# Attention by 512 tokens and four heads instead of 256 tokens and eight heads

## The chip, the cores and the metric

The kernel runs on one core of a Trainium2 chip. The metric is the device time of one execution in microseconds (us).

## What is computed

Attention in chunks of 64 tokens, then a mixture of experts whose router keeps state along the tokens:

```python
# q, k, v: [8 batches, 8 heads, 576 tokens, 64], chunks of 64 tokens
scores = q_c @ k_c.T / 8
attn   = softmax(scores, axis=-1)
x      = (attn @ v_c)  ->  [8, 576, 512]        # heads side by side
logits = x @ w_gate                             # 8 experts
gate   = sigmoid(x @ w_local)
# e = argmax(logits) where s == 0 or gate < 0.5, else the expert of the token before
out[b, s] = softmax(logits)[e] * (relu(x[b, s] @ w1[e]) @ w2[e])
```

## The kernel before

The work has two phases. The attention phase goes over 18 units of 256 tokens by 8 heads. Sixteen are regular (two per batch, tokens 0 to 511, `place`, L117); units 4 and 13 are leftovers, which collect the last 64 tokens of four batches. A unit goes through these steps:

- `load_qk` (L124) brings q and k to SBUF, two consecutive tokens of one head in a row of a partition, so that each contiguous run is 512 bytes; `load_v` (L138) brings v, one token of one head at a time, in runs of 256 bytes, two DMAs for a regular unit and four for a leftover.
- `pair_heads` (L151) copies q and k on GpSimd so that two heads lie side by side (tiles qr, kr).
- `qk_transposes` (L183) turns them with TensorE, four 128x128 blocks to a PSUM bank, and ScalarE moves each bank to qT or kT (L162).
- `scores` (L194): 64 small matmuls into sc; VectorE takes the maximum and subtracts it, ScalarE makes the exponential.
- `p_transposes` (L232), `values` (L241: 64 small matmuls and the division on VectorE), `x_transposes` (L278), each with two or more banks that ScalarE moves.
- `router` (L286): four matmuls for the logits, two transposes, and `red` (L305), which sums on VectorE, copies the nine logits beside x and writes the rows of x with them to DRAM (x_d; 521 floats, 2084 bytes a row).

The order is written out by hand: a string per unit ("steady", L62) names the steps of units at different stages, and each engine runs its part in that order. `lq` issues the load of q and k of unit i+5, `lv` that of v of unit i+1, both on the SP queue, which also carries x_d and the weights and works in order. v has two buffers (L115), so `lv` waits until `values` of unit i-1 has read its buffer. "start" (L41) and "drain" (L45) do the same for the first units and for the change to the second phase; the router's first half (`route`, L337) is hung into units 10 to 15.

The second phase gathers the rows of x by expert in tiles of 128 and runs two matrix multiplications per tile (L684, L705) with weights that are loaded by expert.

Of the kernel before, what the change touches and what calls it, by code (L numbers as in the profile page):

```python
# [32 lines left out]
LEFT = 4  # L33
EARLY = 3
# [27 lines left out]
    "steady": "lq s*8 s h0 tx*8 s va*4 va tq*8 ra*2 h1 tq*8 va*4 lv va ra*2 h2 tp*8 s pr*4 h3 ",  # L62
# [5 lines left out]
def tile_attention_then_moe(ctx: ExitStack, tc, q, k, v, wg, wl, w1, w2, out):  # L68
# [46 lines left out]
    vbuf = [pa1.tile([P, 2, H, DV], F32, name=f"v{i}") for i in range(NV)]  # L115

    def place(i):  # L117
        ph, j = divmod(i, 9)
        if j == LEFT:
            return 9 * ph + 8, [(4 * ph + n, 512, 64) for n in range(4)]  # L120
        j -= j > LEFT
        return 9 * ph + j, [(4 * ph + j // 2, 256 * (j % 2), 256)]

    def load_qk(i, parts=1):  # L124
        qt = pe2.tile([P, H, 2 * D], F32, name="qt", tag="qt", bufs=3)
        kt = pe2.tile([P, H, 2 * D], F32, name="kt", tag="kt", bufs=3)
        p0 = 0
        for b, s0, n in place(i)[1]:
            for h in range(0, H, H // parts):
                for dst, src in ((qt, q), (kt, k)):  # L130
                    nc.sync.dma_start(
                        dst[p0:p0 + n // 2, h:h + H // parts],
                        src[b, h:h + H // parts, s0:s0 + n, :].rearrange("h (p r) d -> p h (r d)", r=2),
                    )
            p0 += n // 2
        return qt, kt

    def load_v(i):  # L138
        vt = vbuf[i % NV]
        t0 = 0  # L140
        for b, s0, n in place(i)[1]:
            for s1 in range(s0, s0 + n, P):
                m = min(P, s0 + n - s1)
                nc.sync.dma_start(
                    vt[t0 % P:t0 % P + m, t0 // P, :, 0:D],
                    v[b, :, s1:s1 + m, :].rearrange("h s d -> s h d"),
                )
                t0 += m
        return vt

    def pair_heads(qk, engs):  # L151
        fns = []
        dsts = [pe2.tile([P, 4, 2, 2, D], F32, name=nm + "r", tag=nm + "r", bufs=1) for nm in "qk"]
        for n in range(2):
            sv = qk[n].rearrange("p (j h) (r d) -> p h j r d", j=2, r=2)
            for r in range(2):
                fns.append(lambda n=n, sv=sv, r=r: evac(engs[2 * n + r], dsts[n][:, :, r], sv[:, :, :, r]))
        return dsts, fns
# [24 lines left out]
    def qk_transposes(hd, qT, kT, engs=None):  # L183
        atoms = []
        fine, engs = engs is not None, engs or QK_ENG
        qkv = [t.rearrange("a h (p r) -> a h p r", r=2) for t in (qT, kT)]
        for m in range(2):
            for r in range(2):
                atoms += trans4(lambda n, m=m, r=r: hd[m][:, n, r].rearrange("p j d -> p (j d)"),
                                [(engs[2 * m + r], qkv[m][:, :, :, r], lambda ps: ps)], fine)  # L190
        return atoms


    def scores(qT, kT, pr, fine=False):  # L194
        sc = ps_s.tile([P, 2, 4, 2, D], F32, name="sc")

        def group(h, cc):
            for cp in range(2):
                ch = 2 * cp + cc
                for j in range(2):  # L200
                    nc.tensor.matmul(  # L201
                        sc[64 * cp:64 * cp + 64, j, h, cc, :],
                        qT[64 * j:64 * j + 64, h, 64 * ch:64 * ch + 64],
                        kT[64 * j:64 * j + 64, h, 64 * ch:64 * ch + 64],
# [36 lines left out]
    def values(pT, vt, xs, fine=False):  # L241
        box = {}

        def group(j, h):
            if h == 0:
                box["o"] = ps_o.tile([P, 2, 512], F32, name="o")
            o = box["o"]
            for cp in range(2):
                for cc in range(2):
                    nc.tensor.matmul(  # L250
                        o[64 * cp:64 * cp + 64, cc, DV * h:DV * h + D + 1],
                        pT[64 * cc:64 * cc + 64, 4 * j + h, 64 * cp:64 * cp + 64],
                        vt[64 * cc:64 * cc + 64, cp, 4 * j + h, 0:D + 1],
                        start=True, stop=True,
                    )
# [3 lines left out]
        def norm(j):  # L259
                ov = box["o"][:, :, 0:4 * DV].rearrange("p c (h d) -> p c h d", d=DV)  # L260
                rs = pa2.tile([P, 2, 4], F32, name="rs")
                nc.vector.tensor_scalar_add(rs, ov[:, :, :, D], 1e-9)
                nc.vector.reciprocal(rs, rs)
                nc.vector.tensor_tensor(
                    xs[:, :, 256 * j:256 * j + 256].rearrange("p c (h d) -> p c h d", d=D),
                    ov[:, :, :, 0:D],
                    rs.unsqueeze(3).to_broadcast([P, 2, 4, D]),
                    ALU.mult,
                )
# [8 lines left out]
    def x_transposes(xs, xT, fine=False):  # L278
        atoms = []
        for cc in range(2):  # L280
            atoms += trans4(
                lambda n, cc=cc: xs[:, cc, P * n:P * n + P],
                [(nc.scalar, xT[:, :, P * cc:P * cc + P], lambda ps: ps)], fine)
        return atoms

    def router(i, xT, xs, fine=False):  # L286
        lg = ps_l.tile([P, 2, 256], F32, name="lg")
        lT = pa2.tile([P, 256], F32, name="lT", bufs=1)

        def mm():  # L290
            for c in range(4):
                nc.tensor.matmul(lg[32 * c:32 * c + 32, 0], wg9[:, c], xT[:, c], start=True, stop=True)
# [6 lines left out]
        def tr():  # L299
            for cc in range(2):  # L300
                nc.tensor.transpose(lg[:, 1, P * cc:P * cc + P], lT[:, P * cc:P * cc + P], ident)
# [3 lines left out]
        def red():  # L305
            slot, rows = place(i)
            Lt = L[:, 2 * slot:2 * slot + 2, :]
# [3 lines left out]
            if len(rows) == 1:  # L311
                (b, s0, n), = rows
                nc.sync.dma_start(x_d[S * b + s0:S * b + s0 + n, :].rearrange("(c p) n -> p c n", p=P), xs)
            else:
                for m, (b, s0, n) in enumerate(rows):
                    nc.sync.dma_start(x_d[S * b + s0:S * b + s0 + n, :], xs[64 * (m // 2):64 * (m // 2) + 64, m % 2])
# [143 lines left out]
    def a_tq(i, engs=None):  # L460
        qkT[i] = (pe2.tile([P, 4, 256], F32, name="qT", bufs=1), pe2.tile([P, 4, 256], F32, name="kT", bufs=1))
        return qk_transposes(hd.pop(i), *qkT[i], engs)

    def a_pair(i, engs=(nc.gpsimd,) * 4):
        hd[i], fns = pair_heads(qk.pop(i), engs)
        return fns

    def a_sa(i, fine=False):
        prs[i] = pa2.tile([P, H, 2, D], F32, name="pr")
        return scores(*qkT.pop(i), prs[i], fine)  # L470
# [5 lines left out]
    def a_va(i, fine=False):  # L476
        xss[i] = pa2.tile([P, 2, XR], F32, name="xs", bufs=3)
        return values(pTs.pop(i), vts.pop(i), xss[i], fine)

    def a_tx(i, fine=False):  # L480
        xTs[i] = pa2.tile([P, 4, 256], F32, name="xT", bufs=1)
        return x_transposes(xss[i], xTs[i], fine)
# [27 lines left out]
    def constants():  # L510
# [10 lines left out]
        for ph in range(2):  # L521
            iota(None, [[9, 4], [4, 2], [2, 2]], base=36 * ph, dst=iota_t[:, TA * ph:TA * ph + TA - 2])
# [22 lines left out]
    for t in vbuf:  # L545
        nc.gpsimd.memset(t[:, :, :, D:DV], 1.0)
# [37 lines left out]
    def slots(pool, q0, q1, halves, qs, tags=({}, {}, {})):  # L584
# [35 lines left out]
        def s3():  # L620
# [9 lines left out]
            V.tensor_single_scalar(bits[:, 0], bits[:, 1], 64, ALU.bitwise_and)  # L630
# [483 lines left out]
```

## Time and profile before

| | us |
|---|---|
| three timed runs: median (lowest to highest) | 669.76 (669.27 to 671.48) |
| the profiled execution, its own time | 674.2 |
| its span, first to last instruction | 672.4 |
| PE busy, of the span | 638.5 (95%) |
| VectorE, ScalarE, GpSimd busy | 371.6, 271.6, 147.1 |

Attention takes about the first 160 us of the span. The profiled execution lies 4.4 us above the median of the timed runs. An engine's busy time is the union of its instructions' spans; the DMA share is the time of all packets over 16 engines, and can pass 1 because packets of one engine overlap.

### The profile page before, as it was taken

To read this page: it belongs to the slowest core of one execution; us is meant where nothing else is said; L and a number is where in the kernel's file an instruction comes from. 1 tells how busy PE (TensorE), PEld (TensorE's weight loads), DVE (VectorE), ACT (ScalarE), POOL (GpSimd) and SP (SyncE) were. 2 spreads that over 40 slices of the span, in tenths; PEclk is the share of its full clock that TensorE was granted. 3 is DMA by queue.
4 is the path that set the end of the run, shared out by engine and by line. 5 is a ranking of instruction groups with operands and counts; after the bars stand their busy time and mean duration, and the time that the engine had idled before them with its cause. 6 is when DMAs were issued, how large, how long until landed. Compare 5 with 4: busy or idle time off the path is not lost. (4 is left out here: it accounts for less than half of the span.)

```text
span 672.4 us, 16746 instructions
## 1 busy us (share of the span) xinstructions
PE 638.5 (95%) x5552; PEld 509.7 (76%) x5552; DVE 371.6 (55%) x938; ACT 271.6 (40%) x434; POOL 147.1 (22%) x209
## 2 busy tenths in 40 slices
PE   4889998889999999999999999999999999999993
PEld 4778776777787888678888886788888888678882
DVE  2656666976783766664332455762377432476231
ACT  4567676655312143542212433531465222342220
POOL 5323353560051111121121121121113121112101
PEclk9899999999999999999999999999999999999997
DMA  9999999977521144235121254452167411144101
GB/s 252 265 263 267 262 268 278 263 221 235 194 100 76 34 158 158 92 110 177 35 64 34 65 175 135 160 153 66 34 212 265 148 45 55 33 160 172 53 19 35
DMA packets 102505, 97.38 MB, mean 145 GB/s; under 512 B 42257, under 2 KB 79121, under 8 KB 102353
## 3 DMA queue, kind: packets, MB, share of 16 engines
q1 hardware_dynamic: 96192, 75.69, 38.8%
q0 software_dynamic: 6160, 19.85, 8.9%
q8 instruction: 73, 1.20, 0.7%
q14 instruction: 80, 0.65, 0.3%
HBM read 76.48 MB, written 19.56 MB: 143 GB/s over the span
## 5 line engine op out<-in xcount | busy, mean ns | idle before, releaser
L705 PE MATMUL y<-w2h,hp 128*128 128x512 f32 x560 | 185.3, 401 | 1.6 <-ACTq L992 1.2
L684 PE MATMUL h<-w1h,xp 128*128 128x512 f32 x560 | 164.3, 403 | 0.0
L771 POOL DMA_INDIRECT out<-ysb,sidx x38 | 43.7, 1151 | 374.0 <-DVEq L976 269.9
L705 PEld LDWEIGHTS y<-w2h,hp 128*128 128x128 f32 x560 | 105.0, 188 | 26.2 <-issue 2.5
L684 PEld LDWEIGHTS h<-w1h,xp 128*128 128x128 f32 x560 | 102.5, 189 | 21.8
L705 PE MATMUL y<-w2l,hp 128*128 128x512 f32 x280 | 110.5, 395 | 0.0
L753 ACT ACTIVATE hsb<-h 128x1024 f32<-128x1024 f32 x35 | 35.9, 1027 | 161.5 <-PE h L684 149.0
L684 PE MATMUL h<-w1l,xp 128*128 128x512 f32 x280 | 88.2, 396 | 0.7 <-DVEq L970 0.7
L652 ACT CAST hp<-tr 128x512 fp32r<-128x512 f32 x76 | 41.2, 589 | 108.1 <-PE tr L650 100.6
L653 DVE TENSOR_TENSOR xp<-tr,xp 128x512 fp32r<-128x512 f32 x39 | 27.0, 691 | 88.2 <-ACTq L970 56.9
L684 PEld LDWEIGHTS h<-w1l,xp 128*128 128x128 f32 x280 | 52.5, 188 | 14.2 <-DVEq L970 1.1
L705 PEld LDWEIGHTS y<-w2l,hp 128*128 128x128 f32 x280 | 52.6, 188 | 11.1
L653 DVE TENSOR_TENSOR hp<-tr,hp 128x512 fp32r<-128x512 f32 x76 | 49.3, 686 | 13.5 <-ACT hp L652 5.7
L1029 DVE TENSOR_SCALAR ysb<-y,ppr 128x512 f32<-128x512 f32 x31 | 23.3, 751 | 32.4 <-PE y L705 31.5
L650 PE MATMUL tr<-ident,hsb 128*128 128x128 f32 x304 | 40.2, 273 | 0.3 <-ACT hsb L753 0.3
L650 PEld LDWEIGHTS tr<-ident,hsb 128*128 128x128 f32 x304 | 35.3, 140 | 6.8 <-ACT w2h L954 1.2
L656 POOL DMA_INDIRECT xg<-x_d,gidx x36 | 35.4, 983 | 21.6 <-issue 9.8
L960 DVE TENSOR_TENSOR w2l<-raw,w2h 128x1024 fp32r<-128x1024 f32 x28 | 33.1, 1223 | 6.5 <-DVEq L943 5.2
L960 DVE TENSOR_TENSOR w1l<-raw,w1h 128x1024 fp32r<-128x1024 f32 x28 | 32.4, 1221 | 6.0 <-ACT w1h L954 5.2
L212 DVE TENSOR_REDUCE mx<-sc 128x8 f32<-128x512 f32 x36 | 23.2, 685 | 20.4 <-PE sc L201 20.4
L954 ACT CAST w2h<-raw 128x1024 fp32r<-128x1024 f32 x28 | 28.6, 1048 | 12.4 <-PE y L711 5.4
L250 PE MATMUL o<-v,pT 64*64 64x65 f32 x1152 | 27.7, 230 | 3.5 <-issue 2.1
(198 smaller groups left out, 833.8 us busy)
## 6 DMA issues: line engine op xcount, KB each, us to landing
raw<-in_moe_w SPq DMA_DIRECT2D x72, 512.0 KB, 4.4
x_d<-xs SPq DMA_DIRECT2D x16, 521.0 KB, 6.2
v<-in_v SPq DMA_DIRECT2D x32, 256.0 KB, 6.4
qt<-in_q SPq DMA_DIRECT2D x15, 512.0 KB, 5.9
kt<-in_k SPq DMA_DIRECT2D x15, 512.0 KB, 6.5
x_d<-xs SPq DMA_DIRECT2D x8, 130.2 KB, 4.2
qt<-in_q SPq DMA_DIRECT2D x8, 128.0 KB, 5.6
kt<-in_k SPq DMA_DIRECT2D x8, 128.0 KB, 4.9
```

What stands on the lines that cost most here:

```text
L250: nc.tensor.matmul(o[64 * cp:64 * cp + 64, cc, DV * h:DV * h + D + 1], pT[64 * cc:64 * cc + 64, 4 * j + h, 64 * cp:64 * cp + 64], vt[64 * ...
L650: nc.tensor.transpose(ps[:, n], src_of(n), ident)
L652: return [tr, lambda: nc.scalar.copy(hi, box["ps"]), lambda: V.tensor_tensor(lo, box["ps"], hi.bitcast(F32), ALU.subtract)]
L653: lambda: V.tensor_tensor(lo, box["ps"], hi.bitcast(F32), ALU.subtract)]
L656: nc.gpsimd.indirect_dma_start(out=dst, out_offset=None, in_=src, in_offset=bass.IndirectOffsetOnAxis(ap=gidx[t].bitcast(U32), axis=0))
L684: nc.tensor.matmul(hs[:, j], xs[a][:, c], W1[w][c][:, 512 * j:512 * j + 512], start=(c == 0 and n == 0), stop=(c == 3 and n == 2))
L705: nc.tensor.matmul(y, hx[f // 4][a][:, f % 4], W2[w][c][:, f % 2, :], start=(f == 0 and n == 0), stop=(f == 7 and n == 2))
L753: nc.scalar.activation(hsb, hs.rearrange("p j f -> p (j f)"), AF.Relu)
L771: nc.gpsimd.indirect_dma_start(out=out, out_offset=bass.IndirectOffsetOnAxis(ap=sidx[t].bitcast(U32), axis=0), in_=ysb, in_offset=None, bo ...
L954: nc.scalar.copy(hi[c], raw[c])
L960: V.tensor_tensor(lo[c], raw[c], hi[c].bitcast(F32), ALU.subtract)
L1029: V.tensor_scalar(ysb, y, pr, None, ALU.mult)
```

## The change

A regular unit is now 512 tokens by four heads; two units (u = 0 and 1) make a batch's 512 tokens. Leftover units stay four batches by eight heads. Four consecutive tokens of one head form a row of q and k (1024 bytes). Transposes come in the order q, k for heads of one half, then q, k for the other; the move from PSUM puts the tokens back in order by its source, not by its destination. v comes by one DMA per head (four for a regular unit) in two steps: `la` (heads 0 and 1) after the first half of `values`, `lv` (heads 2 and 3) after the second. The router adds the two units' partial logits, and each unit writes its half of the rows of x_d. A leftover's x_d goes in two DMAs instead of four.

```diff
-    "steady": "lq s*8 s h0 tx*8 s va*4 va tq*8 ra*2 h1 tq*8 va*4 lv va ra*2 h2 tp*8 s pr*4 h3 ",
+    "steady": "lq s*8 s h0 tx*8 s va*4 la va tq*8 ra*2 h1 tq*8 va*4 lv va ra*2 h2 tp*8 s pr*4 h3 ",
 def load_qk(i, parts=1):
-                        src[b, h:h + H // parts, s0:s0 + n, :].rearrange("h (p r) d -> p h (r d)", r=2),
+        for m in range(parts):
+            for dst, src in ((qt, q), (kt, k)):
+                nc.sync.dma_start(
+                    dst.rearrange("p (h x) -> p h x", h=HU)[:, m:HU:parts],
+                    src[b, HU * u + m:HU * u + HU:parts, 0:8 * CR, :].rearrange("h (p r) d -> p h (r d)", r=4))
 def load_v(i, js=range(2)):
+        for j in js:
+            for h in range(2 * j, 2 * j + 2):
+                nc.sync.dma_start(vh[:, h, :, 0:D],
+                                  v[b, HU * u + h, 0:8 * CR, :].rearrange("(t p) d -> p t d", p=P))
 def pair_heads(i, qk, engs):
+        for m in range(2):
+            for n in range(2):
+                sv = qk[n].rearrange("p (j m r d) -> p m r j d", j=2, m=2, r=4)[:, m]
+                fns.append(lambda n=n, m=m, sv=sv: evac(engs[2 * m + n], dsts[n][:, m], sv))
 def qk_transposes(i, hd, qT, kT, engs=None):
-                                [(engs[2 * m + r], qkv[m][:, :, :, r], lambda ps: ps)], fine)
+            for n, t in enumerate((qT, kT)):
+                atoms += trans4(lambda r, n=n, m=m: hd[n][:, m, r].rearrange("p j d -> p (j d)"),
+                                [(engs[2 * m + n], t[:, 512 * m:512 * m + 512].rearrange("a (p r) -> a p r", r=4),
+                                  lambda ps: ps.rearrange("a r p -> a p r"))], fine)
 def router(i, xT, xs, fine=False):
+                for c in range(2):
+                    xv = xT[:, 512 * c:512 * c + 512].rearrange("a (x s t) -> a s x t", x=2, s=2)
+                    for s in range(2):
...
-            nc.vector.tensor_reduce(
-                Lt, lg[:, 1].rearrange("p (t c e) -> p t e c", t=2, c=4)[:, :, 0:9, :], AX.X, ALU.add)
-            nc.vector.tensor_copy(xs[:, :, C:XR], Lt)
+            if u == 0:
+                for cc in range(2):
+                    nc.vector.tensor_reduce(Lt[:, cc], parts[:, 2 * cc:2 * cc + 2], AX.X, ALU.add)
+            else:
+                nc.vector.tensor_reduce(l2, parts, AX.X, ALU.add)
+                nc.vector.tensor_tensor(lx, Lt, l2.rearrange("p (t g) e -> p t g e", g=2), ALU.add)
+                nc.vector.tensor_copy(Lt, lx)
+            w = CU + u * (E + 1)
+            nc.sync.dma_start(x_d[S * b:S * b + 8 * CR, CU * u:CU * u + w].rearrange("(c p) n -> p c n", p=P),
+                              xv[:, :, 0:w])
```

`scores`, `values` and `x_transposes` change their indices and keep the number and shapes of their instructions; the order of tiles in L, the ids of chunks (iota_t) and the bit operations that turn a slot into a row follow.

## Rows read from the trace of the kernel before

**Rows 1.** The page: busy tenths of PE and DMA in 40 slices of 16.8 us.

```profile
PE   4889998889999999999999999999999999999993
...
DMA  9999999977521144235121254452167411144101
```

**Rows 2.** Windows: us, busy PE PEld DVE ACT POOL, PEclk, DMA share, GB/s.

```profile
0.00:28.00 28.00, 16.60 (x320) 15.09 (x324) 10.83 (x19) 13.27 (x23) 13.46 (x55) 0.94 1.04 253
28.00:160.00 132.00, 121.18 (x2648) 97.57 (x2639) 93.21 (x263) 88.33 (x149) 50.58 (x75) 0.96 0.98 259
```

**Rows 3.** Who PE waited for, 28 to 160 us: us in total, times, longest.

```profile
PE sc L201 <- issue: 5.3, 6, 1.9
PE o L250 <- issue: 2.1, 2, 1.8
PE lg L292 <- issue: 1.5, 1, 1.5
```

**Rows 4.** Timeline around the first stall: start us, us, engine line op.

```profile
43.23 4.12 SPq L144 DMA_DIRECT2D v<-in_v  x4
...
47.16 0.47 PE L201 MATMUL sc<-kT,qT 64*64 64x64 f32 x17 [1.86 <-issue]
```

**Rows 5.** Timeline around two more stalls, and an issue of v without one.

```profile
68.81 0.99 SPq L144 DMA_DIRECT2D v<-in_v  x2
...
70.38 3.07 SPq L316 DMA_DIRECT2D x_d<-xs  x4
...
72.44 0.57 PE L201 MATMUL sc<-kT,qT 64*64 64x64 f32 x22 [1.58 <-issue]
...
128.64 2.58 SPq L313 DMA_DIRECT2D x_d<-xs  x1
...
132.23 0.21 PE L250 MATMUL o<-v,pT 64*64 64x65 f32 x1 [1.77 <-issue]
```

**Rows 6.** Windows behind three stalls, columns as in rows 2.

```profile
48.00:52.00 4.00, 4.00 (x51) 3.31 (x54) 3.21 (x7) 1.68 (x3) 0.04 (x1) 0.62 0.94 230
132.00:138.00 6.00, 5.77 (x65) 4.18 (x64) 4.89 (x17) 2.42 (x4) 6.00 (x11) 0.72 0.23 81
150.00:154.00 4.00, 4.00 (x62) 3.04 (x54) 2.10 (x5) 1.22 (x2) 0.53 (x1) 0.57 1.01 336
```

**Rows 7.** DMA queues (packets, MB, share) in 6:8, then 44:47, then 300:400.

```profile
q1 hardware_dynamic: 1324, 0.67, 111.5%
...
DMA packets 2263, 0.95 MB, mean 315 GB/s; under 512 B 845, under 2 KB 2262, under 8 KB 2262
...
q1 hardware_dynamic: 2262, 0.93, 112.6%
q8 instruction: 1, 0.02, 1.8%
...
q1 hardware_dynamic: 1664, 4.19, 12.6%
```

**Rows 8.** Groups of ACT and DVE, 28 to 160 us: busy us, mean ns.

```profile
L162 ACT COPY pT<-tr 128x512 f32<-128x512 f32 x34 | 18.5, 589 | 14.8 <-PE tr L172 14.8
...
L162 ACT COPY kT<-tr 128x512 f32<-128x512 f32 x28 | 16.4, 642 | 7.5 <-PE tr L172 7.4
...
L212 DVE TENSOR_REDUCE mx<-sc 128x8 f32<-128x512 f32 x30 | 19.3, 685 | 15.9 <-PE sc L201 15.9
L308 DVE TENSOR_REDUCE L<-lg 128x18 f32<-128x72 f32 x14 | 3.1, 223 | 0.0
...
L353 DVE TENSOR_REDUCE mxb<-t 128x18 f32<-128x144 f32 x1 | 0.3, 303 | 0.0
```

**Rows 9.** Page: median us to landing of a 256 KB load; timeline of the start.

```profile
qt<-in_q SPq DMA_DIRECT2D x2, 256.0 KB, 3.0
...
0.74 0.45 SPq L131 DMA_DIRECT2D qt<-in_q  x1
...
6.53 1.94 PE L172 MATMUL tr<-ident,qr 128*128 128x128 f32 x8 [6.53 <-ACT qr L162]
...
27.07 1.18 POOL L164 COPY qr<-qt 128x512 f32<-128x512 f32 x2 [3.17 <-DMA qt<-in_q]
```

More of the change, by code (lines that the diff above doesn't have):

```diff
@@ L33 @@
 LEFT = 4
+HU = H // 2
+CU = C // 2
 EARLY = 3
@@ L114, in tile_attention_then_moe @@
     NV = 2
-    vbuf = [pa1.tile([P, 2, H, DV], F32, name=f"v{i}") for i in range(NV)]
+    vbuf = [pa1.tile([P, 16 * DV], F32, name=f"v{i}") for i in range(NV)]
     def place(i):
@@ new lines, in load_qk @@
+        kt = pe2.tile([P, 8 * P], F32, name="kt", tag="kt", bufs=3)
+        ph, b, u = place(i)
+        if b is None:
+            for n in range(4):
+                for dst, src in ((qt, q), (kt, k)):
+                    nc.sync.dma_start(dst[32 * n:32 * n + 32].rearrange("p (h x) -> p h x", h=H),
+                                      src[4 * ph + n, :, 8 * CR:S, :].rearrange("h (p r) d -> p h (r d)", r=2))
+            return qt, kt
+        for m in range(parts):
[3 more added lines that the diff above has]
+                    src[b, HU * u + m:HU * u + HU:parts, 0:8 * CR, :].rearrange("h (p r) d -> p h (r d)", r=4))
@@ L136, in load_qk, with heads, load_v @@
         return qt, kt
-    def load_v(i):
+    def heads(vt, i):
+        return vt.rearrange("p (h t d) -> p h t d", d=DV, h=H if place(i)[1] is None else HU)
+    def load_v(i, js=range(2)):
         vt = vbuf[i % NV]
[L140 to L148, printed above, removed]
+        vh = heads(vt, i)
+        ph, b, u = place(i)
+        if b is None:
+            for n in range(4 if 1 in js else 0):
+                nc.sync.dma_start(vh[CR * (n % 2):CR * (n % 2) + CR, :, n // 2, 0:D],
+                                  v[4 * ph + n, :, 8 * CR:S, :].rearrange("h s d -> s h d"))
+            return vt
+        for j in js:
+            for h in range(2 * j, 2 * j + 2):
+                nc.sync.dma_start(vh[:, h, :, 0:D],
+                                  v[b, HU * u + h, 0:8 * CR, :].rearrange("(t p) d -> p t d", p=P))
@@ L198, in group @@
             for cp in range(2):
-                ch = 2 * cp + cc
+                t0 = 64 * (4 * h + 2 * cp + cc)
                 for j in range(2):
@@ L238, in p_transposes, with values @@
         return atoms
-    def values(pT, vt, xs, fine=False):
+    def values(i, pT, vt, xs, fine=False):
         box = {}
+        left = place(i)[1] is None
+        vh = heads(vt, i)
         def group(j, h):
@@ L290, in mm @@
         def mm():
-            for c in range(4):
-                nc.tensor.matmul(lg[32 * c:32 * c + 32, 0], wg9[:, c], xT[:, c], start=True, stop=True)
+            if b is None:
+                for c in range(4):
+                    nc.tensor.matmul(lg[32 * c:32 * c + 32, 0], wg9[:, c], xT[:, 256 * c:256 * c + 256],
+                                     start=True, stop=True)
+            else:
+                for c in range(2):
+                    xv = xT[:, 512 * c:512 * c + 512].rearrange("a (x s t) -> a s x t", x=2, s=2)
+                    for s in range(2):
+                        k = 2 * s + c
+                        nc.tensor.matmul(lg[32 * k:32 * k + 32, 0].rearrange("a (x t) -> a x t", x=2),
+                                         wg9[:, 2 * u + c], xv[:, s], start=True, stop=True)
             if not fine:
@@ L299, in tr @@
         def tr():
-            for cc in range(2):
-                nc.tensor.transpose(lg[:, 1, P * cc:P * cc + P], lT[:, P * cc:P * cc + P], ident)
+            for x in range(2):
+                nc.tensor.transpose(lg[:, 1, P * x:P * x + P], lT[:, P * x:P * x + P], ident)
             if not fine:
```

144 lines of the change are left out of this document (84 added, 60 removed).

## The prediction

> **What bounds the kernel now.** I read the 40 slices first. In the first seven the DMA engines are full and PE is busy at eight or nine tenths; from the eleventh slice on PE is full and the DMA mostly idle [rows 1]. Nothing in the second phase reads q, k or v, so a gain must come from PE's time in attention, and it reaches the end whole, since PE then has no gap to give.
>
> The windows cut attention in two [rows 2]. Up to 28 us PE is busy 16.60 of 28.00 us: 11.4 idle, while the first loads come in. From 28 to 160 us it is busy 121.18 of 132.00: 10.8 idle, with a DMA share of 0.98. In this window p is moved 34 times [rows 8], two to a unit, so 17 units take 132 us, 7.8 us each, of which PE works 7.1.
>
> The list of waits says what ends the 10.8 us: 8.9 of it (5.3 + 2.1 + 1.5) is "issue", PE waiting for nothing that the profile shows [rows 3]. The timeline shows that it is few long stalls in the middle of a row of equal matmuls, where there is no semaphore to wait for: 1.86 us with 17 of 64 matmuls left [rows 4], 1.58 us with 22 left, 1.77 us before the last of 32 [rows 5]. There are five such places (the fourth is the wait of lg, 1.5 us [rows 3]; the fifth, between 147 and 150 us, comes in four pieces and is the rest). At each, SP is in a DMA issue that takes long, as 4.12 us for v [rows 4], 3.07 and 2.58 for x_d [rows 5]; two issues of v take 0.99 where the queue is not full [rows 5]. And in each of the five an "instruction" packet of 16 KB is on its way, as in the window of the first [rows 7]. My reading: PE's own code arrives by the same 16 DMA engines, and late when they are full. After three of the stalls the clock is granted at 0.62, 0.72 and 0.57 for 4, 6 and 4 us [rows 6], its lower level for a part of that: 4.0 x 0.38 + 6.0 x 0.28 + 4.0 x 0.43 = 4.9 us lost. So the five stalls cost some 8.5 + 4.9 = 13.4 us, 2.7 each.
>
> **The change part by part.** *Rows of 1024 bytes.* In a window with q and k alone 1324 packets took 111.5% of 16 engines for 2 us: 26.9 ns per 512 bytes [rows 7]. In another 845 of 2263 packets are of 256 bytes: 3 x 16 x 1.126 us, less 1417 x 26.9 ns, leaves 18.9 ns for each [rows 7]. Those two sizes, carried on, give 42.9 ns for 1024 bytes; a line from 512 bytes to the weights' packets (201.6 us over 1664 packets, mean 2.5 KB: 121 ns [rows 7]) gives 50.9. I take the middle, 46.9, against 53.8 for two of 512: 6.9 ns (2.9 to 10.9) saved per KB. Sixteen regular units move 1024 KB of q and k each: 16384 x 6.9 ns / 16 engines = 7.1 us of DMA time (3.0 to 11.2). Halved rows of x_d add 4096 packets, each with the 10.9 ns that the two sizes leave as fixed: 2.8 us back. Net 4.3 us (0.2 to 8.4) of the 160, some 3%.
>
> [...]
>
> *What that buys.* The DMA is hardly ever what PE waits for after 28 us, so the 4.3 us don't come off the end. They thin the queue in front of the code fetches, and a leftover's x_d, at which two of the five stalls lie, comes in two DMAs, not four. Ends: no stall goes (0), or all (-13.4); a sixth may come (+2.7), as new issues shift where the queue is full. I take two of five: -5.4.
>
> *The start.* Before, the first pair copy needs both halves of q, and PE begins at 6.53 [rows 9]. Now it needs one load of 256 KB, issued at 0.74 over 0.45, landing 3.0 us later [rows 9]; a copy of 0.64 (kT's price [rows 8]) then ends at 4.8, so PE begins 1.7 us earlier. The start is then paced by loads: GpSimd waits 3.17 us for q of unit 4 at 27.07 [rows 9]; four regular units are ahead of it, 4 x 1024 x 6.9 ns / 16 = 1.8 us less. The two are one gain, not two: -1.7 (0, if another chain sets the start, to -2.5).
>
> *The moves of qT and kT.* They now read PSUM in steps of 512 bytes and write straight; before they read straight and wrote in steps: 642 ns, where p's straight move takes 589 [rows 8]. No row shows ScalarE reading so. The nearest is VectorE's sum of logits, which reads PSUM in steps of 128 bytes: 223 ns for 72 elements. Straight reads take 303 for 144 and 685 for 512 [rows 8], 1.04 ns an element, so 72 should take 303 - 75 = 228: the steps cost nothing. I take 0, between -0.05 us a copy and twice the price, +0.6; ScalarE is busy 88.33 us for 17 units, 5.2 of 7.8 us, so a rise by up to 0.4 us a copy is hidden there.
>
> [...]
>
> *Small edits.* `red`: for u = 0 two sums for a sum and a copy, for u = 1 one addition more, at most 0.22 us on VectorE per batch. VectorE is busy 93.21 of 132 us and nobody waits for `red` but SP; only the last one stands before the second half of the router: +0.2. v: two more DMA issues, 1.0 us of SP per unit; SP then issues two for q and k, four for v, one for x_d, some 3.5 us of 7.8 at 0.5 each, so hidden as long as the queue isn't full. `la` makes SP wait for the first half of `values`; behind it stand x_d of unit i-2 and `lv`, both later in PE's order anyway, and the load of q and k is ahead of it. It gives half of v a head start, which nobody waits for. GpSimd's pair copies keep size and count. Matmuls keep number and shape: 0.
>
> **Sum:** -5.4 - 1.7 + 0.2 = -6.9, so the profiled execution's 674.2 would become 667.3. It lies 4.4 above the median; taken from the median, 669.76 - 6.9 = 662.9.
>
> **The rivals.** *The queue really empties.* If 3% is enough to keep the fetches in time, all five stalls go: 669.76 - 13.4 - 1.7 + 0.2 = 654.9. For: a share of 0.98 is at the edge, where little moves a lot. Against: a PE without stalls asks 17 units in 118 us instead of 132, so the share would go back up.
>
> *Nothing but the start.* The stalls hang on where PE crosses a page of code, which the same count of instructions leaves in place, and on bursts of DMA that stay; or a run of 1024 bytes is still cut into packets of 512 and the change doesn't do what it says. Then -1.7 to 0: 668.1 to 669.8. For: in the start other chains also show. [...]
>
> *ScalarE becomes the bound.* If the stepped read doubles a move to about 1.2 us, four a unit make 5.2 + 4 x 0.55 = 7.4 us, past PE's 7.1; it decides from 1.1 us a copy on (7.1 - 5.2 = 4 x 0.48). At 1.3 us ScalarE needs 7.8 us a unit, and with the stalls that remain (13.4 / 17 = 0.8) a unit takes 8.6, not 7.8, in the fourteen or so units in which q and k are still turned: +11 - 1.7, some 679. For: no row shows ScalarE at it. Against: VectorE's row.
>
> **The numbers.** Forecast (some stalls go, 657 to 667) 0.45; all go (652 to 657) 0.17; only the start (667 to 671) 0.18; slower by ScalarE or a fuller queue (671 to 685) 0.20. About 0.3%, 2.0 us, is what a measurement of this kernel can tell: below 667.8 is faster, above 671.8 slower. The first two cases and a sliver of the third are faster, 0.64; the rest of the third and the edge of the last same, 0.18; slower 0.18. The range 653 to 675 leaves out the best of the second case and the worse half of the last, about 0.15.
>
> **What would show it.** Right: the packet line with some 12000 packets fewer (16384 of q and k less, 4096 of x_d more); PE's first matmul near 5 us; fewer and shorter "issue" waits in the middle of matmuls, and fewer windows at the lower clock; SP's issues of v nearer 0.5 us each. Wrong: moves of qT and kT well over 0.64 us with PE waiting for ScalarE; the same five stalls in their places; or PE waiting for v, whose loads now come in four pieces.

## The result, and the profile after

The changed kernel is slower: 674.27 us median of five runs (673.69 to 677.11) against 669.27 (668.35 to 671.48) beside it, a ratio of 1.0078 (95% interval 1.005 to 1.0105). Timed again on another chip it gave 676.14 against 672.25, 1.0069 (1.0042 to 1.0096). The profiled execution took 674.83 with a span of 673.0, so unlike that of before it lies at its median. A second trace of the kernel before took 667.81 (span 666.0); it is read beside the first from here on.

The page after: PE and DMA in 40 slices, packets, and the queue of the data [rows 1].

```profile
PE   5888998889999999999999999999999999999994
...
DMA  9999999989623144245111154541158512044201
...
DMA packets 90664, 97.39 MB, mean 145 GB/s; under 512 B 42704, under 2 KB 71376, under 8 KB 90512
...
q1 hardware_dynamic: 84352, 75.70, 39.8%
```

The data queue has 84352 packets, and 96192 before: 11840 fewer, as forecast. But its share did not fall, it rose to 39.8%. The same line of the two traces of the kernel before:

```profile
q1 hardware_dynamic: 96192, 75.69, 38.8%
```

```profile
q1 hardware_dynamic: 96192, 75.69, 38.9%
```

A share times the span is the packets' time on 16 engines: 0.388 x 672.4 = 260.9 us and 0.389 x 666.0 = 259.1 before, 0.398 x 673.0 = 267.9 after. Three more traces of the changed kernel (one unchanged, two that differ in the drain alone) give 265.8 to 268.9. So some 7.9 us more of DMA time, where 4.3 less was forecast. (This is the time that packets were under way. Its share was 1.13 from 68 to 69 us of the first trace of before, so some lie over one another; whether a part of the 7.9 us is packets that held each other up is not shown.)

The windows [rows 2], after:

```profile
0.00:28.00 28.00, 17.91 (x320) 14.39 (x324) 10.82 (x19) 12.80 (x23) 12.50 (x53) 1.00 1.02 246
28.00:160.00 132.00, 118.19 (x2637) 95.22 (x2629) 92.68 (x268) 85.80 (x148) 50.72 (x76) 0.97 0.99 252
```

From 28 to 160 us PE now idles 13.8 us of 132, not 10.8. Who it waited for there [rows 3]:

```profile
PE o L280 <- issue: 3.7, 2, 2.3
PE sc L226 <- issue: 3.2, 4, 1.3
PE o L280 <- DVE xs L302: 2.9, 3, 1.1
PE o L280 <- DMA v<-in_v: 1.8, 1, 1.8
...
PE tr L190 <- issue: 0.6, 1, 0.6
```

"Issue" is 7.5 us with the transposes' 0.6. Before it was 9.4: the 8.9 of the prediction and one more row,

```profile
PE tr L172 <- issue: 0.5, 1, 0.5
```

So a little of the forecast gain is there. In its place stand 1.8 for v, which the prediction had named as a sign of being wrong, and 2.9 for VectorE's division, which in turn waits for room in xs, that is for an x_d to land (VectorE's waits: "DVE xs L302 <- DMA x_d<-xs: 4.0, 3"). The longest "issue" stall and SP's queue, from the timeline [rows 4, 5]:

```profile
60.87 5.67 SPq L157 DMA_DIRECT2D v<-in_v  x4
66.62 1.08 SPq L382 DMA_DIRECT2D x_d<-xs  x1
...
66.94 0.50 PE L280 MATMUL o<-v,pT 64*64 64x65 f32 x17 [2.32 <-issue]
```

Four DMAs of v hold SP for 5.67 us, 1.4 each in the mean, waits included, where the prediction took 0.5, and an x_d stands right behind them. Between 27 and 143 us the longest gap between two issues of SP is 1.7 us (6.1 in the first trace of before, 4.5 in the second).

In the second trace of the kernel before PE's waits are another mix in the same stretch:

```profile
PE o L250 <- DMA v<-in_v: 3.7, 5, 1.2
PE o L250 <- DVE xs L264: 2.0, 3, 1.4
...
PE tr L172 <- issue: 0.6, 1, 0.6
...
PE sc L201 <- issue: 0.4, 2, 0.2
```

1.0 us of "issue" is left there, and 5.7 of waits for v and for VectorE's division have come in. So the five stalls on which the prediction rested are no fixed property of the kernel: they come and go from one execution to the next, and executions of the kernel before ran from 664.87 to 673.48 us on one chip.

### The profile page after: what moved, and what is told of

Read it like the earlier page. It is cut to its first block, busy times and chain, and to the rows that moved or that the text cites. A ratio compares the mean times of both kernels' runs of the same rounds, so it can differ in the third digit from the quotient of the medians.

```text
span 673.0 us, 16813 instructions
## 1 busy us (share of the span) xinstructions
PE 637.7 (95%) x5552; PEld 507.6 (75%) x5552; DVE 371.9 (55%) x946; ACT 269.1 (40%) x434; POOL 147.0 (22%) x209
## 3 DMA queue, kind: packets, MB, share of 16 engines
q1 hardware_dynamic: 84352, 75.70, 39.8%
## 5 line engine op out<-in xcount | busy, mean ns | idle before, releaser
L838 POOL DMA_INDIRECT out<-ysb,sidx x38 | 44.6, 1173 | 373.3 <-DVEq L1044 264.3
L820 ACT ACTIVATE hsb<-h 128x1024 f32<-128x1024 f32 x35 | 35.9, 1027 | 162.6 <-PE h L751 129.7
L751 PEld LDWEIGHTS h<-w1l,xp 128*128 128x128 f32 x280 | 52.5, 188 | 14.1 <-DVEq L1038 1.1
L772 PEld LDWEIGHTS y<-w2l,hp 128*128 128x128 f32 x280 | 52.6, 188 | 11.1
L720 DVE TENSOR_TENSOR hp<-tr,hp 128x512 fp32r<-128x512 f32 x76 | 49.3, 686 | 12.9 <-ACT hp L719 5.4
L717 PEld LDWEIGHTS tr<-ident,hsb 128*128 128x128 f32 x304 | 35.3, 140 | 6.8 <-ACT w2h L1022 1.2
L723 POOL DMA_INDIRECT xg<-x_d,gidx x36 | 35.3, 981 | 21.2 <-issue 9.4
L280 PEld LDWEIGHTS o<-v,pT 64*64 64x64 f32 x1152 | 21.9, 137 | 18.0 <-issue 9.2
L182 POOL COPY qr<-qt 128x512 f32<-128x512 f32 x35 | 21.3, 613 | 63.1 <-issue 46.5
```

The source lines that it names most:

```text
L182: eng.tensor_copy(dst, src)
L280: nc.tensor.matmul(o[64 * cp:64 * cp + 64, cc, col:col + D + 1], pT[64 * cc:64 * cc + 64, 4 * j + h, 64 * cp:64 * cp + 64], vc[64 * cc:64 ...
L717: nc.tensor.transpose(ps[:, n], src_of(n), ident)
L720: lambda: V.tensor_tensor(lo, box["ps"], hi.bitcast(F32), ALU.subtract)]
L723: nc.gpsimd.indirect_dma_start(out=dst, out_offset=None, in_=src, in_offset=bass.IndirectOffsetOnAxis(ap=gidx[t].bitcast(U32), axis=0))
L751: nc.tensor.matmul(hs[:, j], xs[a][:, c], W1[w][c][:, 512 * j:512 * j + 512], start=(c == 0 and n == 0), stop=(c == 3 and n == 2))
```

## Where the time went

One event can be followed in every trace: the first of the two transposes of each unit's router (lg from lT), eighteen times. All times in us; "counted from one", as in some expectations below.

| | first | 14th | 1st to 14th | of it PE idle | granted clock | 15th to last | last |
|---|---|---|---|---|---|---|---|
| before | 35.3 | 144.8 | 109.6 | 8.6 | 0.97 | 14.9 | 173.8 |
| before, second trace | 35.1 | 142.1 | 107.1 | 7.6 | 0.98 | 15.3 | 167.7 |
| after | 35.6 | 149.7 | 114.1 | 12.9 | 0.97 | 16.6 | 176.5 |
| after, second trace (e13) | 35.9 | 150.3 | 114.4 | 13.3 | 0.97 | 16.6 | 180.7 |
| after, other drain (e9) | 35.9 | 145.9 | 110.0 | 9.9 | 0.98 | 16.3 | 172.5 |
| after, other drain (e14) | 36.6 | 145.7 | 109.1 | 11.1 | 1.00 | 15.0 | 173.1 |

The windows of the first and the third line (columns as in [rows 2]):

```profile
35.26:144.85 109.59, 100.99 (x2246) 81.49 (x2240) 78.88 (x224) 74.07 (x126) 43.23 (x66) 0.97 0.99 260
35.61:149.70 114.09, 101.21 (x2242) 81.66 (x2240) 79.39 (x230) 71.98 (x125) 42.65 (x66) 0.97 1.00 247
```

The last four have the same program up to the drain. Mean against mean: the start costs 36.0 - 35.2 = +0.8 us; the steady part 111.9 - 108.3 = +3.6; the gap between the 14th and the 15th router 11.7 - 12.2 = -0.5 (10.2 to 14.1 in single traces); from there to the last 16.6 - 15.1 = +1.5 with the changed kernel's own drain; the second phase (from the fifth gather of x to the end) takes 439.2 to 439.5 against 441.5 and 441.1, -1.9. The sum is +3.5, against +5.0 and +4.6 in the timed runs. Most of the -1.9 lies at the very end: from the start of the last scatter of rows (POOL, L771 and L838) to the end of the span it takes 7.5 and 7.2 us before and 5.7 to 5.9 in the four traces after. In e2 below, which keeps the old tiling, it takes 6.1, so the tiling alone doesn't make it; the cause is open. The steady part's +3.6 is a mean over traces that scatter by 5 us, so the sum is good to some 2 us. But it is all idle time of PE: 11.8 us in the mean of the last four against 8.1, for the same matmuls.

## The experiments

All kernels but e12 and e15 to e18, which are one profiled execution each, are timed against the kernel before in the same rounds; "1.0037 (1.0007 to 1.0067)" is the ratio with its interval. Times of routers and DMA times come from one trace of each kernel. The table says how far routers lie apart in traces of one program; the DMA time of one program differs by up to 3.1 us between traces (265.8 to 268.9 above).

**e1: rows of 1024 bytes alone,** in the kernel before.

```diff
+        if len(place(i)[1]) == 1:
+            (b, s0, n), = place(i)[1]
+            h0 = 4 * (s0 // 256)
...
+                        src[b, h0 + w * m:h0 + w * m + w, 0:512, :].rearrange("h (p r) d -> p h (r d)", r=4))
```

> The kernel before with one edit: q and k of a regular unit are loaded as 512 tokens by four heads in rows of 1024 bytes; everything behind them is as before, so q and k stand at the wrong tokens and heads (the attention weights are those of other tokens). If 1024-byte rows are good for the DMA, as I priced them, DMA time falls by up to 7 us and the time by 1 to 6 us against before (664 to 668). If the rows are themselves what slows the changed kernel, this run shows +2 to +6 us. If DMA time is not what limits, within 1 us of before.

672.92 against 669.48, 1.0037 (1.0007 to 1.0067); the routing is another one and the second phase takes 444.8 us, which is all of the difference. 1st to 14th router 109.0, last at 170.8: attention gains nothing that can be seen beside 109.6 and 107.1. Yet the DMA does gain:

```profile
q1 hardware_dynamic: 79808, 75.69, 37.9%
```

0.379 x 672.6 = 254.9 us, 5.1 less than the 260.0 of before. The forecast of what longer rows save held (7.1, at least 3.0); it buys nothing here.

**e2: x_d in two column halves alone,** in the kernel before.

```diff
-                nc.sync.dma_start(x_d[S * b + s0:S * b + s0 + n, :].rearrange("(c p) n -> p c n", p=P), xs)
+                for c0, c1 in ((0, 256), (256, XR)):
+                    nc.sync.dma_start(x_d[S * b + s0:S * b + s0 + n, c0:c1]...
```

> The kernel before with one edit: each regular unit's rows of x_d go out in two DMAs, columns 0 to 255 and 256 to 520. If halved rows of x_d (and the SP issue more per unit) are the cost, +2 to +6 us against before; if not, within 1.5 us.

671.7, 1.0029 (0.9997 to 1.006); 1st to 14th 110.0, last 170.9. DMA time 0.396 x 668.1 = 264.6 us: 4.6 more, where 2.8 was forecast. PE now waits for v (2.9 us in 28 to 178), which the first trace of before doesn't show and the second does (3.7).

**e3 and e4: v in one step,** without `la`, by head; and in four DMAs of 128 tokens by four heads.

```diff
-    "steady": "... s va*4 la va tq*8 ...
+    "steady": "... s va*4 va tq*8 ...
+        for t in range(4):     # e4 alone
+            nc.sync.dma_start(vh[:, :, t, 0:D],
+                              v[b, HU * u:HU * u + HU, P * t:P * t + P, :].rearrange("h s d -> s h d"))
```

> The changed kernel with v in one step (all four heads at the later place, no la). If SP standing at la is what hurts (x_d and the loads behind it late), this is 2 to 5 us faster than the changed kernel, near 670. If the earlier half of v was a help, 0 to 4 us slower, 674 to 678. If the four DMAs themselves cost, no difference: 673 to 675.

> The changed kernel with v in one step as in the run beside it, in four DMAs of 128 tokens by four heads instead of four of one head by 512 tokens: same count, bytes and 256-byte packets. If the order by head (steps of 32 KB between a partition's packets) is what costs, 2 to 5 us faster than one step by heads; if only count and size of the DMAs matter, the same as that within 1.5 us.

674.8, 1.0066 (1.0037 to 1.0095), and 673.62, 1.0064 (1.0033 to 1.0095). Neither the second step nor the way v is cut makes a difference that can be told from the changed kernel.

**e5: v in four DMAs,** in the kernel before.

```diff
-                nc.sync.dma_start(vt[t0 % P:t0 % P + m, t0 // P, :, 0:D], v[b, :, s1:s1 + m, :]...
+                for h in range(0, H, hs):
+                    nc.sync.dma_start(vt[t0 % P:t0 % P + m, t0 // P, h:h + hs, 0:D], v[b, h:h + hs, s1:s1 + m, :]...
```

> The kernel before with one edit: v of a regular unit comes in four DMAs (128 tokens by four heads) instead of two (128 tokens by eight heads), at the same place, with the same 256-byte packets. If the count and size of the v loads are the cost of the change, +2 to +5 us against before (671.5 to 674.5); if not, within 1 us.

674.28 against 673.32, 1.0009 (0.9993 to 1.0025); 1st to 14th 106.5. Twice as many DMAs of v cost next to nothing there.

**e6, e7: the changed kernel with v in one step of two DMAs of 256 KB, and with whole rows of x_d.** Both write wrong rows or values, as the expectations say.

```diff
+            nc.sync.dma_start(vo[:, t, :, 0:D], v[b, :, s1:s1 + P, :].rearrange("h s d -> s h d"))          # e6
+            nc.sync.dma_start(x_d[r0:r0 + 256, :].rearrange("(c p) n -> p c n", p=P), xs[:, 0:2 * XR]...    # e7
```

> The changed kernel with v in one step and in two DMAs of 128 tokens by eight heads, as before: v stands at the wrong tokens and heads, so the router sees other x and the second phase has other tiles; the end of attention is what is to be compared. If two DMAs less per unit are what matters, the last logits are 3 to 6 us earlier than in the run with one step by heads (181.5) and the run by tokens (177.4), at 172 to 174; if not, 176 to 181.

> The changed kernel, but each regular unit writes 256 whole rows of 2084 bytes to x_d (from its own data, so the rows that the second phase gathers are mixed; the router's choice is unchanged, and so is the number of tiles) and u = 0 makes one small copy more. If halved rows are the cost, 2 to 5 us faster than the changed kernel: 669 to 672; if not, 673.5 to 675.

e6: 669.86 against 673.32, but with another routing, whose second phase takes 432.2 us; its median says nothing on attention. In e6 and e7 the 1st to 14th router take 109.3 and 110.2, as quick as the kernel before, and as the changed kernel at its best; the last router comes at 176.2 and 176.3, as with the changed kernel, after a gap of 14.7 and 14.0 us between the 14th and the 15th. That gap is 10.2 and 13.8 in the two traces of the changed kernel, so neither figure decides. e7 as a whole is 1.0062 (1.0035 to 1.0088). Whole rows take 0.389 x 672.6 = 261.6 us of DMA time, 6.3 less than halves.

**e8: the changed kernel with q and k in rows of 512 bytes** (heads and tokens assigned wrongly).

```diff
-                    src[b, HU * u + m:HU * u + HU:parts, 0:8 * CR, :].rearrange("h (p r) d -> p h (r d)", r=4))
+                    src[b, m:H:parts, 256 * u:256 * u + 256, :].rearrange("h (p r) d -> p h (r d)", r=2))
```

> The changed kernel with q and k in rows of 512 bytes, 256 tokens by eight heads, as before: they stand at the wrong tokens and heads, so the routing and the second phase differ a little; the end of attention is to be compared. If the changed kernel is bound by its DMA engines, longer packets are what it lives on, and without them the last logits come 4 to 9 us later (180 to 186, against 176.5); if it isn't, within 2 us of 176.5.

680.86 against 673.32, 1.0111 (1.009 to 1.0133); 1st to 14th 115.8, DMA time 0.409 x 678.3 = 277.4 us, 9.5 more. Its waits from 28 to 160 us:

```profile
PE o L280 <- DMA v<-in_v: 7.1, 6, 2.4
PE o L280 <- DVE xs L302: 4.3, 5, 1.3
PE sc L226 <- issue: 2.0, 4, 0.7
```

PE waits 7.1 us for v, where the changed kernel waits 1.8. But PE idles 12.8 us between the 1st and the 14th router, and 12.9 and 13.3 in the two traces of the changed kernel: the mix of waits is another one, their sum is not. The ratio's interval overlaps that of the changed kernel (1.005 to 1.0105). That the row length which bought nothing in e1 is needed here is likely, and not shown.

**e9: another order in the drain.** Two waits stand in the changed kernel's timeline:

```profile
163.47 0.33 PE L190 MATMUL tr<-ident,xs 128*128 128x128 f32 x1
163.64 0.38 PE L352 MATMUL lg<-ident,lT 128*128 128x128 f32 x2
164.79 0.33 PE L190 MATMUL tr<-ident,xs 128*128 128x128 f32 x1 [0.77 <-DVE xs L302]
...
171.96 0.33 PE L190 MATMUL tr<-ident,xs 128*128 128x128 f32 x1 [0.68 <-DVE xs L302]
```

The same two transposes before, without a wait:

```profile
162.85 0.27 PE L172 MATMUL tr<-ident,xs 128*128 128x128 f32 x1
...
169.21 0.33 PE L172 MATMUL tr<-ident,xs 128*128 128x128 f32 x1
```

The second turn (transpose) of x reads token tile 1, heads 0 and 1. The program has it wait for the division of heads 2 and 3: the two halves of a unit now lie interleaved over four token tiles (265 floats each), so their address ranges overlap, and a reader of the one waits for the writer of the other. This reason is read from the kernel's addresses; the run below tests the wait, not the reason.

```diff
-        ... tx1 va1 ra2 tx1 m0 w tx1 ...  tx0 va0*3 ra1 va0 tx0 p0 m0 tx0*3 ...
+        ... tx1 va1 ra2 m0 tx1 w tx1 ...  tx0 va0*3 ra1 va0 p0 m0 tx0 tx0*3 ...
```

> The changed kernel with two tokens of the drain string exchanged: the second turn of x of units 16 and 17 (token tile 1), which waits for VectorE's division of the second pair of heads, comes behind the six 512-column matmuls of an early tile, not ahead of them. Theory (the waits at 164.79 and 171.96, 0.77 and 0.68 us, are real stalls of PE that come from the new tiling, since a turn needs one half of xs but the halves' address ranges now interleave): both waits vanish, the last unit's router comes 1.2 to 1.6 us earlier behind unit 14, and the time falls by 1 to 1.6 us against the changed kernel, to a ratio of 1.005 to 1.006 against the kernel before. Rival (PE loses the time anyway, at the next wait, for q of the early tiles or for VectorE): the waits go to other rows and the ratio stays at 1.008.

671.4 against 669.43, 1.0042 (1.0008 to 1.0075). Both waits are gone:

```profile
161.94 0.38 PE L190 MATMUL tr<-ident,xs 128*128 128x128 f32 x2
...
169.37 0.93 PE L190 MATMUL tr<-ident,xs 128*128 128x128 f32 x7
```

In this trace the 15th to last router take 16.3 us, since an "issue" stall of 0.89 us at 166.25 came in; in the next trace of the same kernel (e14) they take 15.0, and in e11 14.9. The gap from the 16th to the 17th router shows it best: 10.5 or 10.6 us in six traces with the changed kernel's own drain (12.0 in e3), 8.9 in five with the other drain (9.8 in e9), 8.8 and 9.2 in the two of the kernel before. So the waits are worth some 1.7 us.

**e10: both undone,** the drain and the smaller pieces of v and x_d (e6, e7 and e9 together).

> The changed kernel with the drain of the run before, v in two DMAs of 256 KB in one step (heads and tokens assigned wrongly, so the values and the routing are other ones) and x_d in whole rows of 2084 bytes (also wrong rows). The 1024-byte rows of q and k, the units of 512 tokens and all matmuls stay. Theory (the loss is the smaller DMAs of v and x_d in the steady part, plus the drain): units 1 to 14 take 106 to 110 us, as with the kernel before, the last router comes by 172 us, where the kernel before has 170.8 to 173.8 and the changed one 176.5. Rival (something else in the new tiling costs the time, as the order of the turns or the pair copies): units 1 to 14 take 113 us and the last router comes at 175 or later. The second phase may take a few us more or less since other rows go to other experts; it is left out of the comparison.

665.77 against 669.43, with a second phase of 431.5 us (another routing). 1st to 14th 110.0 and last router at 174.0: between what the two theories said, and no better than the drain alone (172.5 and 173.1). The pieces alone are not shown to be the cause.

**e11: x_d on ScalarE's queue,** with the drain of e9.

```diff
-            nc.sync.dma_start(x_d[S * b:S * b + 8 * CR, CU * u:CU * u + w]...
+            nc.scalar.dma_start(x_d[S * b:S * b + 8 * CR, CU * u:CU * u + w]...
```

> The changed kernel with the drain of the first run of this call and the x_d of regular units issued on ScalarE's DMA queue, not on SP's. Bytes, packets and counts are the same. Theory A (the 16 DMA engines are what is full): nothing changes in the steady part, units 1 to 14 take 113 to 114 us, ratio as that of the first run. Theory B (SP's queue in order is what is full: v and q stand behind an x_d that waits for the router or for room): units 1 to 14 take 107 to 110 us, PE no longer waits for v, and the ratio falls under 1.002. [...]

674.0, 1.0052 (1.0023 to 1.0081); 1st to 14th 115.9. With x_d off SP's queue the steady part is no shorter: the theory of a full SP queue (B) falls. PE waits no longer for v, but 10.9 us for "issue".

**e12: the kernel before again.**

> The kernel before, unchanged, for a second trace of it. Both theories: time 668 to 675; units 1 to 14 take 106 to 110 us and the last router comes 170.8 to 173.8 us after the start, as in the runs that change one thing of it. If the stalls without a visible reason sit where code is fetched, they come behind the same matmuls as in the first trace, with other lengths.

667.81; 107.1 and 167.7, at and beyond the quick end of what was expected, and with hardly an "issue" stall (the waits stand in the first section). The stalls don't come back behind the same matmuls.

**e13, e14: the changed kernel and its drain on one chip.**

> The changed kernel, unchanged, timed beside its drain variant on one chip. Theory (drain 1.5 to 2 us, the rest more stalls of the same kinds): ratio 1.006 to 1.009; units 1 to 14 take 110 to 115 us, the gap between the routers of units 15 and 16 is 10.6 us as before. Rival (the first trace was an unlucky one, and the drain is nearly all of the loss): units 1 to 14 take 107 to 110 us and the ratio is 1.003 to 1.005.

> The drain variant of the run e9 again, beside the changed kernel. Theory: 1.5 to 2.5 us under the changed kernel, ratio 1.003 to 1.006, since the stalls of the steady part stay. Rival: the drain is nearly all of the loss, and the ratio is within 1.0015 of 1.

1.0069 (1.0042 to 1.0096) and 1.0058 (1.0028 to 1.0088), 676.14 and 675.42 against 672.25. The two intervals overlap widely: in time the drain's gain is not told apart from none here. In the traces it is: 16.6 and 15.0 from the 15th router to the last, and 10.5 and 8.9 from the 16th to the 17th (the gap that the expectation names, counted there from nought).

**e15, e16: without v** from unit 2 on, in the drain variant of the changed kernel and in the kernel before.

```diff
-        for j in js:
+        for j in js if i < 2 else ():
```

> The drain variant of the changed kernel without the loads of v of regular units from unit 2 on (the buffers keep what they have, so the values and the routing are other ones). Theory (all that the new tiling loses in the steady part is DMA: pieces, room in the queue): with the DMA share well under 0.9, PE has no stall left, every unit takes its shortest time of the earlier traces (7.2 to 7.3 us in units 2 to 8), and units 1 to 14 take 102 to 106 us, within 1 us of the kernel before without v. Rival (a loss of its own in the order of the turns, the pair copies or the router): units 1 to 14 take over 2 us longer than in the kernel before without v, with PE waiting for VectorE, ScalarE or GpSimd.

> The kernel before without the loads of v of regular units from unit 2 on (other values and another routing). Theory: units 1 to 14 take 102 to 106 us, PE's stalls without a visible reason go with the full queue, and the last router comes by 165 us. Rival (those stalls hang on where code is fetched alone): three or more stalls of over 1 us stay, and units 1 to 14 take 107 to 110 us.

1st to 14th 108.1 and 106.1, with a DMA share of 0.73 and 0.74 from 28 to 160 us. "Issue" stalls of over 1 us stayed in both (1.8 and 2.6; 1.2 and 2.1), so both theories were off: at these mean shares the stalls did not end. The two differ by 2.0 us, where e15's theory said at most 1 and its rival over 2, so this pair doesn't decide on a loss of the tiling's own. The DMA time is 0.331 x 675.6 = 223.6 and 0.329 x 673.6 = 221.6 us: 2.0 apart, where with v it is 7.9.

**e17, e18: without q and k too,** from unit 7 on.

```diff
+        if b is not None and i >= 7:
+            return qt, kt
```

> The drain variant of the changed kernel without the loads of q and k of regular units from unit 7 on and of v from unit 2 on (the buffers keep what they have; other values and another routing). From about 60 us on only x_d, the weights and the leftover loads are left. Theory (code waits for data): between 60 and 140 us the DMA share is under 0.5, no stall of PE ends behind a packet of code, the packets of code take under 0.95 us and the units take their shortest times: from the router of unit 5 to that of unit 14 68 to 72 us. Rival (the stalls belong to the code): stalls of 1 to 2.5 us stay, and those units take over 73 us.

> The kernel before without the loads of q and k of regular units from unit 7 on and of v from unit 2 on (other values and another routing). Theory: as with the changed kernel, within 1 us from the router of unit 5 to that of unit 14, 68 to 72 us, so that the two tilings have the same pace. Rival (the new tiling has a loss of its own beside DMA): it is 2 us or more shorter than the changed kernel.

From the 5th to the 14th router 72.0 us (changed) and 73.0 (before): the same pace in both tilings. The window from 60 to 140 us and what PE waited for in it, in the changed kernel:

```profile
60.00:140.00 80.00, 76.09 (x1742) 62.38 (x1735) 64.83 (x190) 56.63 (x100) 37.35 (x56) 0.98 0.31 90
```

```profile
PE o L283 <- DVE xs L305: 2.9, 2, 2.5
PE tr L446 <- ACT pT L183: 0.7, 1, 0.7
PE tr L491 <- DVE oh L486: 0.2, 1, 0.2
```

and in the kernel before:

```profile
60.00:140.00 80.00, 76.36 (x1735) 62.69 (x1724) 63.69 (x184) 57.99 (x99) 37.65 (x56) 0.96 0.28 90
```

```profile
PE o L253 <- DVE xs L267: 2.7, 1, 2.7
PE tr L379 <- ACT pT L165: 0.8, 1, 0.8
```

With the DMA at a share of 0.31 and 0.28, no "issue" stall is left in 80 us in either, and no wait for v. What remains is the same in both (VectorE, at the router's first half). So in this pair of traces the new tiling has no loss of its own in the steady part: what it loses there it loses with the DMA share at 0.99 (its own trace, 28 to 160 us).

## Why the prediction was wrong

**The reading of the stalls holds as far as the traces go.** They show packets of 16 KB in a queue named "instruction" (73 in the trace of after), and that the stalls go with them: over 20 traces there are 80 "issue" stalls of 0.5 us or more between 28 and 180 us, and 74 of them end 1.2 to 1.75 us behind the landing of such a packet; a moment taken at random lies so behind one 8 or 9 times in 100. In the timeline above, such a packet started at 64.57 and took 0.93 us; PE went on at 66.94, 1.44 us later. That the packets carry PE's own code, and that PE waits for it, is the author's reading: the profile names no engine for them. e17 and e18 fit its other half, that the stalls come where the DMA is full: none is left at shares of 0.31 and 0.28 (60 to 140 us). That the packets come late there is not shown: those of the five stalls took 0.88 to 1.01 us, and those of the second phase 0.95 to 1.08 in the medians of the traces. One reading beside it was not right: the issue of v in 0.99 us was put down to a queue that is not full [rows 5], but the DMA share was 1.13 and 1.14 just then (68 to 69 and 69 to 70 us), so a short issue of v is no sign that the engines have room.

**The step that failed is "What that buys".** It took five stalls of one execution for a property of the kernel and let two of them go, -5.4 us, for 3% less DMA time. Three things were wrong in it. First, a second trace of the kernel before has nearly none of them, and waits for v instead; PE idles 7.6 us from the 1st to the 14th router there and 8.6 with the five stalls. What PE waits for changes from one trace to the next (9.4 us of "issue" in the first; in the second 1.0, and 5.7 for v and the division). e1 shows what less DMA time buys: 5.1 us of it gone, attention the same. Second, the profiled execution of before lay 4.4 us above its median, and its stalls were taken as those of the median. Third, the DMA time did not fall. In place of 5.4 us less, PE's idle time in the steady part rose by 3.7 us (8.1 to 11.8 in the mean), and the whole went up by 5.0, not down by 6.9. That 674.27 still lies in the range of 653 to 675 is no merit: the range took in the nearer half of the slower case, which the prediction held for unlikely (0.20).

**The clock term**, 4.9 of the 13.4 us, was put on the same stalls. From 28 us on the granted clock stood at 0.5 for 3.4 us three times in the first trace of before (from 47.6, 133.0 and 150.0 us), and once in the second:

```profile
86.60:90.00 3.40, 3.40 (x44) 2.69 (x44) 1.07 (x3) 0.96 (x2) 0.26 (x1) 0.50 1.02 228
```

Before this one PE had waited 1.24 and 1.03 us for v, and not for "issue". So a fall came behind waits for v too. Its price, 3.4 x 0.5 = 1.7 us, is an estimate that lets PE's pace go with the clock; in the first of these stretches eight transposes took 1.93 us and 32 matmuls of o 1.15, and behind it, at 1.00, they took 1.09 (at 52.34) and 0.70 (at 53.36). By that estimate the clock makes 3.4 of the 6.1 us up to the last router between the two traces of before; between the tilings it makes next to nothing in the steady part (0.97 and 0.98 against 0.97, 0.97, 0.98 and 1.00 in the table).

**The DMA terms.** Rows of 1024 bytes: forecast -7.1 us (3.0 to 11.2), measured -5.1 in the kernel before (e1) and -9.5 in the changed one (e8): right. That is the packets' time; that more bytes pass in a second at 1024 bytes the runs don't show (from the 1st to the 14th router 257 GB/s in e1, 260 and 272 before). Halves of x_d: forecast +2.8, measured +4.6 (e2) and +6.3 (e7): mis-sized, at 1.6 and 2.3 times the forecast, perhaps because the 10.9 ns a packet were worked out from two sizes in windows of loads alone. v by head was costed as 1.0 us of SP and no DMA time; the changed kernel's 7.9 us more shrink to 2.0 where v is left out (e15, e16), so some 5.9 go with v, or with the fuller DMA (share 0.99 with v, 0.73 without). Which part of its loads that is stays open: v in four DMAs cost the kernel before 0.392 x 669.2 - 260.0 = 2.3 us (e5), less than traces of one program differ by, and v in two DMAs saved the changed kernel nothing (e6: 0.402 x 665.5 = 267.5).

**The start** was forecast at -1.7. PE does begin at 4.40 us instead of 6.53 [rows 9], but by 28 us it has done the same 320 matmuls as before, which only took 1.3 us longer (17.91 and 16.60 us [rows 2]), and the first router comes 0.3 us later (0.8 in the mean of four traces). The bound named there, 0 if another chain sets the start, was passed to the other side. The DMA share in this stretch is 1.02 after and 1.04 before, at 246 and 253 GB/s [rows 2], and the longer rows alone bring the first router no sooner (36.3 in e1); which chain sets it wasn't tested.

**"Matmuls keep number and shape: 0"** missed a wait: the drain's 1.7 us. The prediction looked at what the instructions cost and not at whom they wait for once the layout of xs had changed.

**Right, at a cost of zero:** the moves of qT and kT. ScalarE's groups from 28 to 160 us, after [rows 8]:

```profile
L180 ACT COPY pT<-tr 128x512 f32<-128x512 f32 x34 | 18.4, 589 | 17.1 <-PE tr L190 17.1
...
L180 ACT COPY kT<-tr 128x512 f32<-128x512 f32 x28 | 16.5, 595 | 2.0 <-PE tr L190 1.8 <-ACT qT L180 0.2
L180 ACT COPY qT<-tr 128x512 f32<-128x512 f32 x28 | 16.4, 594 | 21.0 <-PE tr L190 21.0
```

594 ns with the stepped read of PSUM, 642 before with the stepped write, 589 straight. The rival in which ScalarE becomes the bound is false. The slower side that came true was the one half-named beside that rival: a fuller queue (7.9 us more of packets' time). `red` is as cheap as forecast: two sums of 184 ns for u = 0. No engine waits for it; SP does, as the prediction had it: 6.3 us behind 165 us (SP's waits: "SPq L382 <- DVE L L380: 6.3, 2, 3.6"), and 5.9 before (L310, from 28 to 180 us).

What stays open is which of the new transfers of v and x_d makes the steady part 3.6 us longer, and how much of that is luck of the traces. A rival is left too: the "instruction" packets themselves take longer in the changed kernel (last section), and no run takes that apart from the data. That the loss is gone at DMA shares of 0.31 and 0.28, so that it is not the tiling's work on the engines, is what the last two runs show, with one trace each.

## What to carry to other kernels

Before stalls are priced, look at a second execution: those of one trace are a sample. Here one trace of the kernel before had 9.4 us of "issue" and the next 1.0, with PE idle for 8.6 and 7.6 us from the 1st to the 14th router; and where the changed kernel had 1.9 us less of it, 4.7 of waits for v and the division stood in its place. When the layout of a tile changes, follow each of its readers to the writer whose addresses now overlap; a cheaper order of two steps may be all that is needed (here it was worth some 1.7 us). Smaller transfers can cost the DMA more than longer rows elsewhere give back (here 7.9 us more of packets' time in all, though the rows of 1024 bytes saved 5.1 and 9.5), so the sum is made for every transfer of the stage, those that are only re-cut too.

## What the runs showed of the hardware

- Packets of 16 KB in a queue named "instruction" go over the same 16 DMA engines as the data (73 packets, 0.8% of the engines' time, in the trace of after). Of PE's 80 "issue" stalls of 0.5 us or more, 74 end 1.2 to 1.75 us behind the landing of one. At mean DMA shares of 0.73 and 0.74 such stalls of up to 2.6 and 2.1 us stay; at 0.31 and 0.28 none is left from 60 to 140 us (one trace of each tiling).
- These packets take longer in the changed kernel: in the median from 28 to 150 us 1.09 to 1.25 us in twelve of the thirteen traces of it and its variants (1.04 in one without v), 0.95 to 1.03 in the seven of the kernel before and its variants. In the second phase they take the same, 0.95 to 1.08. The light pair differs too (1.11 and 0.97), so it is not the load alone; no run explains it.
- One kernel's executions scatter by 1.3% on one chip (664.87 to 673.48 us, 29 runs). Of the 6.4 us between the two traces of before 6.1 lie ahead of the last router, with the DMA share at 0.98 from 28 to 160 us of the first; 3.4 of them are the granted clock's by the estimate of 1.7 us for each 3.4 us at 0.5.
